# Second stage of a convolution and spectral-mixing kernel: eight single banks, the two array halves a step apart, and the last mixing groups in separate banks

## The chip, the cores and the metric

The kernel runs on one core of one Trainium2 chip. The metric is the device time of one execution in microseconds (us); the median of three runs of the kernel before is 186.36 us (186.29 to 186.38).

## The reference

`x` has 8 batches, 3264 positions and 192 channels; all is float32 at the interface. Each of eight channel groups gets a causal convolution of seven taps (a softmax of `weight`). The result is then mixed in the frequency domain: its lowest 64 frequencies are multiplied by one complex 192 x 192 matrix each, transformed back and added; last comes a channel product with a ReLU.

```python
out = np.einsum('hk,bskhg->bshg', softmax(weight), x_unf)      # causal conv, 7 taps
X = np.fft.rfft(out, axis=1)[:, :64]
Yr = einsum('bmd,mde->bme', Xr, w_r) - einsum('bmd,mde->bme', Xi, w_i)
Yi = einsum('bmd,mde->bme', Xr, w_i) + einsum('bmd,mde->bme', Xi, w_r)
y = np.fft.irfft(Y, n=3264, axis=1)
u = out + y
return u + np.maximum(u @ w_ch, 0.0)
```

## The kernel before

The schedule is written out by hand: each engine executes its instructions in the order of the text, and a library places the semaphores.

The front part loads `x` through GpSimd's queue, convolves it on TensorE with banded matrices (`conv_pass`, line 299), adds and subtracts the two half sequences (`fold`), and transforms them to 64 frequencies (`dft`, `xtrans`). Transposed copies of the convolved rows go to `ct`, cosine and sine tables to `gtab`.

Mixing goes over 16 groups of four frequencies. `mix(g)` (line 472) multiplies by the group's matrices, which stream in through GpSimd's queue into a ring of buffers; twelve small products go to one of two banks `sums`, two groups side by side in a bank. After each second group `mix_copy` (line 479, ScalarE) takes both out to `ymix`, `mix_trans` transposes them (line 485) into a bank of `ye`, and two copies (line 491 on VectorE, 493 on ScalarE) scatter them into `yet`. `keep_busy` (line 570) issues products whose results nobody reads.

The second stage works on 52 items `(q, kk)`: a pair `q` of batches and a block `kk` of 2 x 128 positions. In an item, `a` is 0 or 1 for even and odd positions; each `a` has a PSUM bank of 384 columns (two batches of 192 channels). Into each bank go, for `u @ w_ch`,

- "c": three products of 192 columns, the transposed rows `ct` by the channel matrix (`wa`, `wb`),
- "g": one product of 384 columns, the table `gtab` by `zw[0]`, the mixed spectrum already multiplied by `w_ch`,

then the ReLU in place (`relu`, line 545, ScalarE), then

- "y": one product of 384 columns, `gtab` by `zw[1]`, the mixed spectrum itself, added to the clamped values,

and at last `finish` (line 551, VectorE) adds the convolved rows, writes to one of seven buffers `outs`, and a store goes out on SyncE's queue (line 561).

Every one of these products uses 64 of the array's 128 rows. Half of the terms lie in the lower 64 rows (`row` 0) and half in the upper 64 (`row` 1), so that two products run at once. The two halves must not write to one bank at the same time. `both(n, first, which)` (products on line 538) therefore issues pairs: the lower half adds to bank `first`, the upper half to the other bank of the item; later the halves change banks. Where they change, a wait on TensorE's own semaphore is put ahead (the "turn"). An item holds two banks, so four items are in PSUM at once (`Z[n % 4]`, two tiles named `outleft` and two `outright`). The order per step is

```python
both(n, 0, "c", begin=True); both(n, 0, "g")
both(n - 2, 1, "y", end=True); finish(n - 2)
both(n, 1, "c"); both(n, 1, "g"); relu(n)
both(n - 1, 0, "y")
```

The spectrum times `w_ch` and the spectrum itself, `zw`, are computed by `zw_pair(q, ...)` (lines 498, 499: 384 columns, first 128 rows, then 64) and scaled out by VectorE (line 504) and ScalarE (506). Pairs 0 and 1 come before the first item, pairs 2 and 3 between the first items. The "c" products of items 0 and 1 are issued ahead, while the last two mixing groups wait for weights.

Of the kernel before, what the change touches and what calls it, by code (L numbers as in the profile page):

```python
# [9 lines left out]
ALU = mybir.AluOpType  # L10
# [9 lines left out]
def kernel(  # L20
# [443 lines left out]
    ye = hand_out("right", "mix", (1, 1))  # L464
    trans_banks(2)

    def mix(g):
        yp = sums[(g // 2) % 2][:, D * (g % 2):D * (g % 2) + D]
        for j in range(3):
            for p4 in range(4):  # L470
                m = 8 * (g // 2) + g % 2 + 2 * p4
                nc.tensor.matmul(yp[32 * p4:32 * p4 + 2 * B, :], xt[:, j, :, m],  # L472
                                 wbuf(g)[:, p4, j, :], start=(j == 0), stop=(j == 2),
                                 tile_position=(0, 32 * p4), skip_group_check=True)
        if g >= NWC:
            load_w(g + NWA)

    def mix_copy(d):
        nc.scalar.copy(out=ymix[d % 2][:], in_=sums[d % 2][:, 0:2 * D].rearrange("p (g d) -> p g d", g=2))

    def mix_trans(d):
        et = ye[d % 2][:, :].bitcast(BF16)[:, 0:4 * P].rearrange("p (t g k) -> p t g k", t=2, g=2)
        for t in range(2):
            for g in range(2):
                nc.tensor.transpose(et[:, t, g, :], ymix[d % 2][:, g, 64 * t:64 * t + P], ident[:])
        for t in range(2):
            dst = yet[:, t, :, :].rearrange("p b (r c j) -> p r c b j", r=2, c=2)[:, :, :, :, 4 * d:4 * d + 4]
            srcv = et[:, t, :, :].rearrange("p g (q k) -> p g q k", q=4)[:, :, :, 0:16].rearrange(
                "p g q (c b) -> p g c b q", c=2)
            if t == 0:  # L490
                nc.vector.tensor_copy(out=dst, in_=srcv)
            else:
                nc.scalar.copy(out=dst, in_=srcv)

    def zw_pair(q, zt, engines):
        for i in range(2):
            b = 2 * q + i
            nc.tensor.matmul(zt[:, i, 0:2 * D], yet[:, 0, b, :], wa[:], start=True, stop=False)  # L498
            nc.tensor.matmul(zt[:, i, 0:2 * D], yet[64:P, 1, b, :], wb[64:P, :], start=False, stop=True)  # L499
        for i in range(2):  # L500
            dst = zw[:, :, 2 * q + i, :]
            srcv = zt[:, i, 0:2 * D].rearrange("p (t d) -> p t d", t=2)
            if engines[i] == "v":
                nc.vector.tensor_scalar(out=dst, in0=srcv, scalar1=ascale[:, 0:1], scalar2=None, op0=ALU.mult)  # L504
            else:
                nc.scalar.activation(out=dst, in_=srcv, func=ACT.Copy, scale=ascale[:, 0:1])  # L506

    Z = []
    items = [(q, kk) for q in range(NQ) for kk in list(range(1, NS)) + [0]]
    N = len(items)  # L510

    def pieces(n, a, row, which):
        q, kk = items[n]
        r = slice(64 * row, 64 * row + 64)
# [9 lines left out]
    def both(n, first, which, begin=False, end=False):  # L524
        zt = Z[n % 4]
        lists = (pieces(n, first, 0, which), pieces(n, 1 - first, 1, which))
        old = held.get(n % 4)
        if old is not None and old[0] != first and not begin:
            nop = nc.tensor.nop()
            for name in old[1]:  # L530
                tc.add_manual_dep(nop.ins, name, mybir.DependencyInfo(mybir.DependencyClass.Sync,
                                                                      mybir.DependencyReason.DATA),
                                  reason="row tiles take turns on a bank")
        last = [None, None]
        for k in range(len(lists[0])):
            for row in range(2):
                cols, l, r = lists[row][k]
                m = nc.tensor.matmul(zt[:, first ^ row, cols], l, r, start=(begin and k == 0),  # L538
                                     stop=(end and k == len(lists[row]) - 1), skip_group_check=True)
                last[row] = m.ins.name  # L540
        held[n % 4] = (first, last)

    def relu(n):
        z = Z[n % 4][:, :, 0:2 * D]
        nc.scalar.activation(out=z, in_=z, func=ACT.Relu)  # L545

    def finish(n):
        q, kk = items[n]
        zt = Z[n % 4]
        o = outs[n % NO]  # L550
        nc.vector.tensor_tensor(out=o[:, :, :, :].rearrange("p i a d -> p a i d"),  # L551
                                in0=zt[:, :, 0:2 * D].rearrange("p a (i d) -> p a i d", i=2),
                                in1=c_rows(q, kk), op=ALU.add)
# [9 lines left out]
    def c_ahead(n):  # L563
        for first in range(2):
            both(n, first, "c", begin=(first == 0))

    def keep_busy(n, bank):

# [1 line left out]
            nc.tensor.matmul(sums[bank][:, 0:2 * D], ident[:], xall[:, 0, 0, 0:2, :], start=True, stop=True,  # L570
                             skip_group_check=True)

    AHEAD = 2
    for g, beside in enumerate((0, 1, 1, 2, 2, 2, 1, 2, 2, 2, 2, 2, 2, 2, 0, 0)):
        d = g // 2
        mix(g)
        if g == NG - 2:
            Z += hand_out("left", "out", (2, 2))
            c_ahead(0)
            keep_busy(5, 0)  # L580
        if g == NG - 1:
            mix_copy(d)
            c_ahead(1)
            mix_trans(d)
            keep_busy(4, 0)
        elif g % 2:
            mix_copy(d)
            trans_banks(beside)
            mix_trans(d)
        else:  # L590
            trans_banks(beside)
        if g == NG - 3:
            trans_banks(len(tjobs))
        if NG // 2 <= g < NG - 2:
            keep_busy(3, 1 - d % 2)
    stacks.pop("right").close()
    stacks.pop("sum").close()
    Z += hand_out("right", "out", (2, 2))
    zw_pair(0, Z[2], "va")
    zw_pair(1, Z[3], "va")  # L600
    for n in range(N + 2):
        if n < N:
            if n >= AHEAD:
                both(n, 0, "c", begin=True)
            both(n, 0, "g")
        if 0 <= n - 2 < N:
            both(n - 2, 1, "y", end=True)
            finish(n - 2)
        if n < N:
            if n >= AHEAD:  # L610
                both(n, 1, "c")
            both(n, 1, "g")
            relu(n)
        if n == 1:
            zw_pair(2, Z[2], "va")
        if 0 <= n - 1 < N:
            both(n - 1, 0, "y")
        if n == 1:
            zw_pair(3, Z[3], "va")
    for side in ("right", "left"):  # L620
        stacks[side].close()

# [29 lines left out]
```

## Time and profile before

| | us |
|---|---|
| median of three runs | 186.36 |
| the profiled execution | 186.3 |
| its span, first to last instruction | 184.5 |
| TensorE busy | 157.1 |
| VectorE busy | 119.1 |
| ScalarE busy | 108.7 |

The granted TensorE clock is 0.986 on average over the span. PE is TensorE's products, PEld its weight loads, DVE VectorE, ACT ScalarE, POOL GpSimd, SP SyncE. A timeline row gives start, duration (several instructions that follow each other are merged), engine, line, operation, output and inputs, shapes, count, and in brackets the idle time before it and what ended it. Matrix products are pipelined: a record's duration reaches from its start to the end of the last column's way through the array, and the next product on the same rows starts well before that.

### The profile page before, as it was taken

Reading aid. Unit: us, or ns where it says so; the run is one execution under the profiler, and the core shown is the slowest. Engines: PE = TensorE matmul, PEld = TensorE weight load, DVE = VectorE, ACT = ScalarE, POOL = GpSimd, SP = SyncE. Lnnn points to the kernel's source line nnn. Section 1 sums busy time; section 2 is a strip of 40 time slices with the busy share of each in tenths; the row PEclk is TensorE's granted clock in tenths of the full one; section 3 lists DMA queues with packets and bytes.
Section 4 is the critical chain, followed back from the end, with each engine's and each line's share of the span. In section 5 each row is a group of like instructions: output and inputs, shape, how many; then the busy total and the mean of one; then the engine's idle time right before and its main releaser. Section 6 shows DMA issues by size and latency. Waiting matters only on the chain.

```text
span 184.5 us, 6555 instructions
## 1 busy us (share of the span) xinstructions
PE 157.1 (85%) x2841; PEld 117.1 (63%) x2841; DVE 119.1 (65%) x185; ACT 108.7 (59%) x155; POOL 64.4 (35%) x106
## 2 busy tenths in 40 slices
PE   0064997599999999899998889999999999999970
PEld 0053996499899898678765532566666666666630
DVE  3883865546868866965443303678777877778780
ACT  6367474358686686568645315566666666666640
POOL 7977999576756653332252000000000000000000
PEclk9999999879999999999999999999999999999997
DMA  3999999999999999999999900188879888798884
GB/s 20 176 189 190 190 194 187 191 191 192 191 192 189 202 205 208 204 207 207 209 203 208 171 7 0 66 322 317 326 277 358 319 295 335 290 342 319 319 338 156
DMA packets 50320, 40.14 MB, mean 218 GB/s; under 512 B 29044, under 2 KB 50292, under 8 KB 50292
## 3 DMA queue, kind: packets, MB, share of 16 engines
q0 software_dynamic: 36208, 19.67, 77.5%
q1 hardware_dynamic: 14084, 20.06, 29.6%
q8 instruction: 22, 0.36, 0.8%
q14 instruction: 6, 0.05, 0.1%
HBM read 39.33 MB, written 20.05 MB: 322 GB/s over the span
## 4 chain that ended last, share of the span: by engine, by line
DMA 40%; PE 37%; POOL 14%; issue 4%; DVE 1%; ACT 1%; POOLq 0%; DVEq 0%
DMA xall<-in_x_dram 18%; PE outright L538 17%; PE outleft L538 17%; DMA arena<-in_moe_w_i_dram 12%; DMA ct<-in_moe_w_i_dram 11%; POOL xall L154 10%; POOL ct L280 1%; DVE mixa L504 1%; ACT mixa L506 1%; PE outright L498 1%; PE outright L499 1%; DVE arena L551 1%; PE sumright L472 1%; POOL wa L247 0%; POOL perm L247 0%
## 5 line engine op out<-in xcount | busy, mean ns | idle before, releaser
L299 PEld LDWEIGHTS <-band 128*64 128x64 bf16 x944 | 40.0, 123 | 19.1 <-ACT band L219 11.0
L299 PE MATMUL cvleft<-xall,band 128*64 128x192 bf16 (+4 forms) x640 | 31.9, 254 | 14.7 <-ACT band L219 11.0
L154 POOL DMA_DIRECT2D xall<-in_x_dram x48 | 36.0, 762 | 8.6 <-DMA xall<-in_x_dram 7.3
L538 PEld LDWEIGHTS <-ct 64*128 64x128 bf16 x624 | 24.5, 94 | 21.9 <-PE outleft L538 7.5
L538 PE MATMUL outleft<-mixa,gtab 64*128 64x384 bf16 x208 | 32.0, 323 | 0.5 <-ACT mixa L506 0.3
L538 PE MATMUL outright<-mixa,gtab 64*128 64x384 bf16 x208 | 31.8, 323 | 0.4 <-ACT outright L545 0.3
L323 ACT CAST xall<-cvleft 128x768 bf16<-128x768 f32 (+3 forms) x29 | 21.5, 756 | 10.5 <-PE cvleft L299 10.3
L328 DVE TENSOR_TENSOR arena<-xall 128x1536 bf16<-128x1536 bf16 (+1 forms) x28 | 22.5, 844 | 7.9 <-ACT xall L323 7.5
L545 ACT ACTIVATE outright<-outright 128x768 f32<-128x768 f32 x26 | 20.7, 795 | 10.8 <-PE outright L538 10.8
L545 ACT ACTIVATE outleft<-outleft 128x768 f32<-128x768 f32 x26 | 20.6, 794 | 10.2 <-PE outleft L538 10.2
L551 DVE TENSOR_TENSOR arena<-outright,xall 128x768 f32<-128x768 f32 x23 | 22.0, 958 | 5.7 <-ACT outleft L545 2.9
L551 DVE TENSOR_TENSOR arena<-outleft,xall 128x768 f32<-128x768 f32 x22 | 21.1, 958 | 5.8 <-ACT outright L545 2.6
L375 DVE COPY ct<-trleft 128x1024 bf16<-128x1024 bf16 (+1 forms) x19 | 12.4, 663 | 15.4 <-PE trleft L406 8.7
L538 PEld LDWEIGHTS <-gtab 64*128 64x128 bf16 x416 | 18.9, 94 | 2.6 <-issue 1.1
L538 PE MATMUL outright<-wa,ct 64*128 64x192 bf16 x208 | 17.4, 245 | 0.2 <-ACT mixa L506 0.2
L538 PE MATMUL outleft<-wa,ct 64*128 64x192 bf16 x208 | 17.4, 245 | 0.1
L299 PE MATMUL cvright<-xall,band 128*64 128x192 bf16 (+4 forms) x304 | 15.6, 245 | 1.9 <-DVE xall L321 1.2
L373 ACT COPY ct<-trleft 128x1024 bf16<-128x1024 bf16 x13 | 13.2, 1013 | 5.1 <-PE trleft L403 3.0
L323 ACT CAST xall<-cvright 128x768 bf16<-128x768 f32 (+3 forms) x13 | 9.8, 751 | 8.6 <-PE cvright L299 8.4
L403 PEld LDWEIGHTS <-xall 128*128 128x128 bf16 x208 | 11.7, 98 | 2.6 <-issue 0.3
L538 PE MATMUL outright<-wb,ct 64*128 64x192 bf16 x104 | 12.8, 243 | 0.0
L538 PE MATMUL outleft<-wb,ct 64*128 64x192 bf16 x104 | 12.8, 243 | 0.0
(107 smaller groups left out, 189.5 us busy)
## 6 DMA issues: line engine op xcount, KB each, us to landing
out_dram<-arena SPq DMA_DIRECT2D x41, 384.0 KB, 3.3
xall<-in_x_dram POOLq DMA_DIRECT2D x48, 192.0 KB, 7.8
out_dram<-band SPq DMA_DIRECT2D x7, 384.0 KB, 3.9
ct<-in_moe_w_r_dram POOLq DMA_DIRECT2D x8, 288.0 KB, 9.1
ct<-in_moe_w_i_dram POOLq DMA_DIRECT2D x8, 288.0 KB, 10.0
arena<-in_moe_w_r_dram POOLq DMA_DIRECT2D x8, 288.0 KB, 10.1
arena<-in_moe_w_i_dram POOLq DMA_DIRECT2D x8, 288.0 KB, 11.0
out_dram<-arena SPq DMA_DIRECT2D x8, 144.0 KB, 2.4
```

The costliest lines, as they stand in the source:

```text
L154: nc.gpsimd.dma_start(out=xall[:, q, t % 2, k:k + 4, :], in_=src)
L280: nc.gpsimd.dma_start(out=wbuf(g)[64 * half:64 * half + 64, :, :, :], in_=src[m0:m0 + 7:2, :, :].rearrange("m (p j) e -> p m j e", j=3))
L299: nc.tensor.matmul(o, bd3[:, h, c0:c0 + P - 1:2], xall[:, q, t, ks:ks + n, GRP * h:GRP * h + GRP], start=(main and a == 0), stop=not main, ...
L323: nc.scalar.copy(out=dst, in_=srcv)
L328: nc.vector.tensor_tensor(out=cpm[:, r, :, 0:2 * nb, :], in0=src[:, :, :, 0, :], in1=src[:, :, :, 1, :], op=op)
L373: nc.scalar.copy(out=out, in_=in_)
L375: nc.vector.tensor_copy(out=out, in_=in_)
L403: nc.tensor.transpose(o, cv[:, blk, 0:P], ident[:])
L472: nc.tensor.matmul(yp[32 * p4:32 * p4 + 2 * B, :], xt[:, j, :, m], wbuf(g)[:, p4, j, :], start=(j == 0), stop=(j == 2), tile_position=(0, ...
L538: m = nc.tensor.matmul(zt[:, first ^ row, cols], l, r, start=(begin and k == 0), stop=(end and k == len(lists[row]) - 1), skip_group_check ...
L545: nc.scalar.activation(out=z, in_=z, func=ACT.Relu)
L551: nc.vector.tensor_tensor(out=o[:, :, :, :].rearrange("p i a d -> p a i d"), in0=zt[:, :, 0:2 * D].rearrange("p a (i d) -> p a i d", i=2), ...
```

## The change

- The eight banks of the second stage are single tiles. Its unit is no longer the item with two banks but the slot, an item's `a`, with one bank (`Z[s % 8]`); there are 104 of them.
- Within a slot the lower half puts in c and g first, then the upper half; then the ReLU; then y from the lower half and y from the upper half. The order among slots is worked out at build time by `second_stage`, which keeps times for both halves, VectorE and ScalarE and always issues the product that can start first. In the steady part the lower half is then at slot s with c and g while the upper half is at slot s - 1, the lower y at s - 3 and the upper y at s - 4.
- ReLU, add and eviction are done per slot, on 384 columns instead of 768. A store still takes a whole item, except for the last item: each half goes out alone, the second from ScalarE's queue.
- The weights `zw` of the first pair are computed by `zw_first` in three banks, 192 columns at a time and on all 128 rows (the lower rows of `yet[:, 1]` are set to zero at the start by one memset). Those of the other six batches are six more slots between the items, each with one wide product on the lower half and two on the upper.
- The last two mixing groups go to different banks of `sums`. The first of the two is copied out (ScalarE) and transposed before the other arrives; the other is copied out by VectorE. Their transposes go to both banks of `ye`, so the two copies into `yet` read different banks. Four c slots are issued ahead as before.
- The short item `kk = 0` is no longer the last of a pair but the third from the end.

```diff
+            nc.vector.memset(yet[0:64, 1, :, :], 0.0)
...
+    def mix_bank(g):
+        return sums[(g // 2 + (g == NG - 1)) % 2]
...
-    def zw_pair(q, zt, engines):
+    def zw_first(q, banks):
+        def part(o, i, t):
+            cols = slice(D * t, D * t + D)
+            nc.tensor.matmul(o, yet[:, 0, 2 * q + i, :], wa[:, cols], start=(t == 0 or i == 0), stop=False, ...)
+            nc.tensor.matmul(o, yet[:, 1, 2 * q + i, :], wb[:, cols], start=False, stop=True, ...)
         for i in range(2):
+            part(banks[i][:, 0:D], i, 0)
+        for i in range(2):
+            part(banks[2][:, D * i:D * i + D], i, 1)
+        for i in range(2):
+            scaled(zw[:, 0, 2 * q + i, :], banks[i][:, 0:D], "va"[i])
+        scaled(zw[:, 1, 2 * q:2 * q + 2, :], banks[2][:, 0:2 * D]..., "v")
...
-    items = [(q, kk) for q in range(NQ) for kk in list(range(1, NS)) + [0]]
+    NZ = 8
+    items = [(q, kk) for q in range(NQ) for kk in list(range(1, NS - 2)) + [0, NS - 2, NS - 1]]
+    slots = [(n, a) for n in range(len(items)) for a in range(2)]
+    for k, b in enumerate(range(2, B)):
+        slots.insert(9 + 5 * k, (None, b))
+    NC = 4
...
+    def product(s, row, piece, start, stop):
+        old = held.get(s % NZ)
+        if old is not None and not start and old[0] != row:
+            nop = nc.tensor.nop()
+            tc.add_manual_dep(nop.ins, old[1], ..., reason="row tiles take turns on a bank")
+        cols, l, r = piece
+        m = nc.tensor.matmul(Z[s % NZ][:, cols], l, r, start=start, stop=stop, skip_group_check=True)
+        held[s % NZ] = (row, m.ins.name)
...
+    def relu(s):
+        z = Z[s % NZ][:, 0:2 * D]
         nc.scalar.activation(out=z, in_=z, func=ACT.Relu)
...
+        nc.vector.tensor_tensor(out=o[:, :, a, :], in0=Z[s % NZ][:, 0:2 * D]..., in1=c_rows(q, kk)[:, a, :, :], op=ALU.add)
+        if n == len(items) - 1:
+            (nc.scalar if a else nc.sync).dma_start(out=dst, in_=o[:, :, a, :])
+            return
+        if a == 0:
+            return
...
+    TURN, CLAMP, ADD, COPY, SEEN = 560, 1140, 1340, 1400, 750
+
+    def second_stage():
...
+        while ynext[1] < len(yslots):
+            best = None
+            for row in range(2):
...
+                if t is not None:
+                    best = min(best or (1e9,), (max(t, free[row]), 0, row))
+                s, k = at[row]
+                if s < n_slots:
+                    t = 0 if k else (opened if row == 0 else below)[s]
+                    if t is not None:
+                        best = min(best or (1e9,), (max(t, free[row]), 1, row))
...
         if g == NG - 2:
-            Z += hand_out("left", "out", (2, 2))
+            nc.scalar.copy(out=ymix[d % 2][:, 0, :], in_=mix_bank(g)[:, 0:D])
+            Z += hand_out("left", "out", (1, 1, 1, 1))
             c_ahead(0)
-            keep_busy(5, 0)
-        if g == NG - 1:
-            mix_copy(d)
-            c_ahead(1)
-            mix_trans(d)
+            for t in range(2):
+                mix_trans(LAST, t, (0,), ye[1 - t])
             keep_busy(4, 0)
+        elif g == NG - 1:
+            nc.vector.tensor_copy(out=ymix[d % 2][:, 1, :], in_=mix_bank(g)[:, D:2 * D])
+            c_ahead(2)
+            for t in range(2):
+                mix_trans(LAST, t, (1,), ye[1 - t])
+            keep_busy(4, 1)
...
-    Z += hand_out("right", "out", (2, 2))
-    zw_pair(0, Z[2], "va")
-    zw_pair(1, Z[3], "va")
-    for n in range(N + 2):
...
+    Z += hand_out("right", "out", (1, 1, 1, 1))
+    zw_first(0, Z[4:7])
+    second_stage()
```

More of the change, by code (lines that the diff above doesn't have):

```diff
@@ L495, in zw_pair, with mix_trans @@
-    def zw_pair(q, zt, engines):
+    def mix_trans(d, t, groups=(0, 1), bank=None):
+        et = (bank or ye[d % 2])[:, :].bitcast(BF16)[:, 2 * P * t:2 * P * (t + 1)].rearrange("p (g k) -> p g k", g=2)
+        for g in groups:
+            nc.tensor.transpose(et[:, g, :], ymix[d % 2][:, g, 64 * t:64 * t + P], ident[:])
+        if groups[-1] == 0:
+            return
+        rows = slice(64 * t, P)
+        dst = yet[rows, t, :, :].rearrange("p b (r c j) -> p r c b j", r=2, c=2)[:, :, :, :, 4 * d:4 * d + 4]
+        srcv = et[rows, :, :].rearrange("p g (q k) -> p g q k", q=4)[:, :, :, 0:16].rearrange(
+            "p g q (c b) -> p g c b q", c=2)
+        if t == 0:
+            nc.vector.tensor_copy(out=dst, in_=srcv)
+        else:
+            nc.scalar.copy(out=dst, in_=srcv)
@@ new lines, in scaled @@
+    def scaled(dst, srcv, engine):
+        if engine == "v":
+            nc.vector.tensor_scalar(out=dst, in0=srcv, scalar1=ascale[:, 0:1], scalar2=None, op0=ALU.mult)
+        else:
+            nc.scalar.activation(out=dst, in_=srcv, func=ACT.Copy, scale=ascale[:, 0:1])
+    def zw_first(q, banks):
+        def part(o, i, t):
+            cols = slice(D * t, D * t + D)
+            nc.tensor.matmul(o, yet[:, 0, 2 * q + i, :], wa[:, cols], start=(t == 0 or i == 0), stop=False,
+                             skip_group_check=True)
+            nc.tensor.matmul(o, yet[:, 1, 2 * q + i, :], wb[:, cols], start=False, stop=True,
+                             skip_group_check=True)
@@ L513, in pieces @@
+    slots = [(n, a) for n in range(len(items)) for a in range(2)]
+    for k, b in enumerate(range(2, B)):
+        slots.insert(9 + 5 * k, (None, b))
+    NC = 4
+    def pieces(s, row, which):
+        n, a = slots[s]
+        r = slice(64 * row, 64 * row + 64)
+        if n is None:
+            sides = ((0, wa),) if row == 0 else ((0, wa), (1, wb))
+            return [(slice(0, 2 * D), yet[r, t, a, :], w[r, :]) for t, w in sides]
         q, kk = items[n]
-        r = slice(64 * row, 64 * row + 64)
@@ L522 @@
     held = {}
[L524 to L528, printed above, removed]
-            nop = nc.tensor.nop()
[L530 to L547, printed above, removed]
+    def product(s, row, piece, start, stop):
+        old = held.get(s % NZ)
+        if old is not None and not start and old[0] != row:
+            nop = nc.tensor.nop()
+            tc.add_manual_dep(nop.ins, old[1], mybir.DependencyInfo(mybir.DependencyClass.Sync,
+                                                                    mybir.DependencyReason.DATA),
+                              reason="row tiles take turns on a bank")
+        cols, l, r = piece
+        m = nc.tensor.matmul(Z[s % NZ][:, cols], l, r, start=start, stop=stop, skip_group_check=True)
+        held[s % NZ] = (row, m.ins.name)
@@ new lines, in c_ahead, with second_weights @@
+    def c_ahead(s0):
+        for first in range(2):
+            for k in range(3):
+                for row in range(2):
+                    s = s0 + (first ^ row)
+                    product(s, row, pieces(s, row, "c")[k], first == 0 and k == 0, False)
+    def relu(s):
+        z = Z[s % NZ][:, 0:2 * D]
+        nc.scalar.activation(out=z, in_=z, func=ACT.Relu)
+    def second_weights(s, engine):
+        q, i = divmod(slots[s][1], 2)
+        scaled(zw[:, :, 2 * q + i, :], Z[s % NZ][:, 0:2 * D].rearrange("p (t d) -> p t d", t=2), engine)
@@ L588 @@
             trans_banks(beside)
-            mix_trans(d)
+            for t in range(2):
+                mix_trans(d, t)
         else:
```

113 lines of the change are left out of this document (62 added, 51 removed).

## The prediction

> **What bounds the kernel now.** I read the chain of work that ended last, then the timeline of the table stage by engine, its start and its end.
>
> ```profile
> DMA 40%; PE 37%; POOL 14%; issue 4%; DVE 1%; ACT 1%; POOLq 0%; DVEq 0%
> 107.69 0.46 PE L472 MATMUL sumright<-arena,mixa 128*16 128x192 bf16 x12 [0.63 <-DMA arena<-in_moe_w_i_dram]
> 117.24:177.08 59.84, 59.84 (x986) 39.45 (x982) 46.94 (x49) 39.28 (x50) 0.00 (x0) 1.00 0.84 310
> GB/s 20 176 189 190 190 194 187 191 191 192 191 192 189 202 205 208 204 207 207 209 203 208 171 7 0 66 322 317 326 277 358 319 295 335 290 342 319 319 338 156
> ```
>
> Transfers and their issues (DMA, POOL) bound the front part: PE still waits for weights when the last mixing starts at 107.69. Up to there the change only adds one memset on VectorE, which the chain does not touch. From about 108 us PE carries the chain. In the steady stretch (the third row, a stretch's length and then PE, PEld, DVE, ACT, POOL, clock, DMA share, GB/s) 49 adds take 59.84 us, 1.22 us for an item; DVE is busy 46.94 and ACT 39.28 of it, and the clock is full. One period of PE:
>
> ```profile
> 141.08 0.33 PE L538 MATMUL outright<-mixa,gtab 64*128 64x384 bf16 x2
> 141.24 0.33 PE L538 MATMUL outleft<-mixa,gtab 64*128 64x384 bf16 x2
> 141.47 0.34 PE L538 MATMUL outright<-wa,ct 64*128 64x192 bf16 x4
> 141.65 0.25 PE L538 MATMUL outright<-wb,ct 64*128 64x192 bf16 x2
> 141.73 0.33 PE L538 MATMUL outright<-mixa,gtab 64*128 64x384 bf16 x2
> 141.89 0.33 PE L538 MATMUL outleft<-mixa,gtab 64*128 64x384 bf16 x2
> 142.06 0.33 PE L538 MATMUL outright<-wa,ct 64*128 64x192 bf16 x4
> 142.22 0.25 PE L538 MATMUL outright<-wb,ct 64*128 64x192 bf16 x2
> 142.30 0.33 PE L538 MATMUL outright<-mixa,gtab 64*128 64x384 bf16 x2
> ```
>
> Products come in pairs, lower and upper half of the array at once. A wide pair (384 columns) occupies its halves for 0.163 us (141.08 to 141.24, 141.73 to 141.89), three narrow pairs (192) for 0.245 (142.06 to 142.30). An item is six narrow and four wide pairs: 2 x (0.245 + 2 x 0.1625) = 1.14 us. The other 0.08 us of the 1.22 sit in one place: from 141.24 + 0.16 to 141.47 the array waits for a turn. The wide pair that began at 141.08 must be through before the other half may add to its bank at 141.47, 0.39 us start to start, and only one wide pair lies in between. After that wait three narrow pairs take 0.26 instead of 0.245: about 0.01 to load weights that could not be loaded ahead.
>
> **The change, part by part.** *Steady stage.* A slot is half an item: one bank, three narrow and two wide products on each half of the array, 0.570 us. The built order staggers the halves. The lower half runs c, c, c, table, relu'd table; the upper half enters the bank one slot later and finishes its relu'd product (y) four slots later. Two turns stay in each slot. For the first, a lower wide y (0.163) and one narrow product lie between, so the upper half starts 0.39 - 0.325 = 0.065 us behind the lower and keeps that offset. For the second, three narrow products on the lower half cover 0.16 + 0.245 = 0.41 against 0.39. Both are covered with almost nothing to spare, so the 0.08 us per item goes, and 0.01 us of reloading per turn may remain: between 0 and 2 x 0.01 x 104 = 2.1 us. I take 0.8, because a half that falls behind finds its turn done and its weights loaded.
>
> Behind a waiting weight load, all later products of both halves are queued, so this must fit in both. The rest of the loop has room: from a slot's first product to its free bank it is about 0.41 + 0.23 + 0.41 + 0.21 + 0.48 + 0.05 + 0.16 + 0.23 + 0.16 + 0.27 + 0.56 = 3.2 us of products, turns, relu and add, and eight banks give 8 x 0.57 = 4.6.
>
> ```profile
> 61.09 0.95 DVE L321 CAST xall<-cvright 128x768 bf16<-128x768 f32 x1
> 61.95 0.68 DVE L375 COPY ct<-cvleft 128x1024 bf16<-128x1024 bf16 x1
> L321 DVE CAST xall<-cvright x5: 558/958/1158, 16.9 to 65.7; 128x768 bf16<-128x768 f32 x3, 128x384 bf16<-128x384 f32 x1, 128x960 bf16<-128x960 f32 x1
> 141.67 0.96 DVE L551 TENSOR_TENSOR band<-outleft,xall 128x768 f32<-128x768 f32 x1 [0.26 <-ACT outleft L545]
> ```
>
> *Adds and relus in halves.* No 384-element add is in the trace. The L321 cast out of PSUM takes 0.558 at 384 and 0.958 at 768, and the add takes 0.96 at 768, so I take 0.56 for a half add: 104 x 0.56 = 58.2 us on DVE, up 8 us from 52 x 0.96. A half relu I put at the 0.48 us of ACT's 128x384 copy (below), 50 us in all. Both fit within a slot of 0.57, DVE barely; but a DVE instruction that is ready starts before its predecessor's record ends (61.95 against 61.09 + 0.95), so its own limit is nearer 0.47.
> The Trainium skill (TensorEngine Tiling (Array Packing), PSUM Bottleneck) says the opposite of this edit: after a tiling speedup the PSUM copies may become the bound, and accesses should be vectorised across tiles. The trace agrees that the fixed part is paid twice (2 x 0.558 for 0.958) and does not show the pace; by the rule DVE would set it, which is a rival below.
>
> *Halves out of step.* Row tiles run only in lockstep in this trace. The nearest rows are column tiles: 16 products in step, and 16 whose second half trails (the 4th to 5th ends step by 0.05, not 0.08 or 0):
>
> ```profile
> 63.08 0.83 PE L299 MATMUL cvright<-xall,band 128*64 128x192 bf16 x16
> 64.80 0.36 PE L299 MATMUL cvright<-xall,band 128*64 128x192 bf16 x4
> 64.80 0.41 PE L299 MATMUL cvright<-xall,band 128*64 128x192 bf16 x5
> 64.80 0.85 PE L299 MATMUL cvright<-xall,band 128*64 128x192 bf16 x16
> ```
>
> 0.85 against 0.83: staggering costs the lag once. Bounds for row tiles: nothing, or up to a narrow product's 0.03 us per slot if each entry costs a reload (3 us). I take nothing, since the column rows are the nearest. The Trainium skill (same page, Key Properties) says that tiles work independently and load weights and multiply in parallel, which gives the same zero; no row here shows it for row tiles.
>
> *From the last weights to the first table product.*
>
> ```profile
> 108.74 0.25 PE L538 MATMUL outleft<-wb,ct 64*128 64x192 bf16 x2
> 108.92 0.40 PE L485 MATMUL mixright<-ident,ymix 128*128 128x128 bf16 x4
> 109.15 0.81 PE L570 MATMUL sumright<-xall,ident 128*128 128x384 bf16 x4
> 110.12 0.32 PE L498 MATMUL outright<-wa,yet 128*128 128x384 bf16 x1
> 110.37 0.33 PE L499 MATMUL outright<-wb,yet 64*128 64x384 bf16 x1
> ...
> 112.63 0.34 PE L538 MATMUL outleft<-mixa,gtab 64*128 64x384 bf16 x2 [0.33 <-ACT mixa L506]
> ```
>
> ```profile
> 108.25 0.48 ACT L479 CAST ymix<-sumright 128x384 bf16<-128x384 f32 x1 [3.56 <-PE sumright L472]
> 109.68 0.27 ACT L493 COPY yet<-mixright 128x128 bf16<-128x128 bf16 x1 [0.95 <-DVE yet L491]
> 112.00 0.58 ACT L506 ACTIVATE mixa<-outright,ascale 128x384 bf16<-128x384 f32 x1 [2.06 <-DVE mixa L504]
> ```
>
> ```profile
> 109.36 0.29 DVE L491 COPY yet<-mixright 128x128 bf16<-128x128 bf16 x1 [4.42 <-PE mixright L485]
> 111.35 0.62 DVE L504 TENSOR_SCALAR mixa<-outright,ascale 128x384 bf16<-128x384 f32 x1 [1.70 <-PE outright L499]
> ```
>
> Before, this takes 112.63 - 107.69 = 4.94 us. The copy of the mixed half shortens (0.36 on DVE, estimated from the slope of L321, for 0.48 on ACT), but PE is on its early products until 108.8, so the transposes stay at 108.92. Two of them instead of four: the filler L570 starts 0.11 earlier and ends at 109.69. The two copies into `yet`, which followed each other on one bank (109.36, 109.68), run side by side in two and end by 109.55. So the weights' first product starts at 109.7 instead of 110.12. It was a train of 384-column products at 0.26 apart (110.12, 110.37), alternating between 128 and 64 rows; now it is 192 columns on all 128 rows, some 0.08 apart as in the filler's 0.16 for 384. Two banks are done at 110.2; half-width copies (0.62 - 0.20 and 0.58 - 0.16 = 0.42) run in parallel and end at 110.7; the first table product starts at about 110.8. That is 1.86 us earlier; with the copies still one after the other 1.4.
>
> *Other weights between items.* The two pairs in the middle of the old stage become six slots on row tiles: one wide product below, two above, 12 x 0.1625 = 1.95 us on the upper half, the longer one.
>
> *End.*
>
> ```profile
> 177.14 0.89 PE L538 MATMUL outright<-mixa,gtab 64*128 64x384 bf16 x6
> 177.51 0.80 ACT L545 ACTIVATE outright<-outright 128x768 f32<-128x768 f32 x1 [0.43 <-PE outright L538]
> 178.36 0.73 PE L538 MATMUL outright<-mixa,gtab 64*128 64x384 bf16 x4 [0.32 <-ACT outright L545]
> 178.13 2.02 DVE L551 TENSOR_TENSOR arena<-outright,xall 128x768 f32<-128x768 f32 x2
> 180.15:184.54 4.39, 0.00 (x0) 0.00 (x0) 0.00 (x0) 0.00 (x0) 0.00 (x0) 0.79 0.45 152
> out_dram<-arena SPq DMA_DIRECT2D x41, 384.0 KB, 3.3
> out_dram<-arena SPq DMA_DIRECT2D x8, 144.0 KB, 2.4
> ```
>
> After the last upper table product: 0.17 until it is through, 0.04 to ACT (177.14 + 0.33 against 177.51), relu 0.48, 0.05 back (177.51 + 0.80 against 178.36), a turn 0.39: 1.13 us. After the last y 0.17, 0.10 to DVE (141.24 + 0.33 against 141.67) and an add of 0.56: 0.83. From the last add (178.13 + 2.02 = 180.15) to the end it was 4.39 us with two small stores issued in a row. Now one 192 KB store from ACT's queue comes last, between the two rows of stores (2.4 and 3.3 us), in pieces half as long: +0.1, from -0.3 to +0.5.
>
> *Sum, first table product to last add:* 100 slots x 0.570 + 4 x 0.325 (their early products are done) = 58.3; weights 1.95; the first turn 0.39; stalls while the first slots fill, walked through the order, 0.5 (0.2 to 1.0); reloads 0.8; 1.13; 0.83. Together 63.9, before 180.15 - 112.63 = 67.5: 3.6 less. In all -1.86 - 3.6 + 0.1 = -5.4: span 184.5 to 179.2. The profiled run took 186.3, 1.8 beside its span, which gives 180.9; the median is 0.06 above that run: **181.0 us**.
>
> **Rivals.** *Turns not covered (slower).* The place is the weight load of the upper half, twice in a slot. If a turn takes more than 0.39 when the other half keeps running, everything behind it waits. One gap like the old one (0.08) in every slot costs 104 x 0.077 - 0.8 = 7.2: 188.2. The point is 5.3/104 = 0.05 us per slot. For it: no spare. Against it: the same wait was 0.39 in each period. Chance 0.10.
> *Evictions bind (slower),* the skill's rule as a mechanism: if a half add can neither overlap its predecessor nor have its wait done ahead, its pace is 0.56 + 0.10 = 0.66, 0.08 over my slot: +8.5, 189.5; the point is a pace of 0.63. Against it stands the 61.09/61.95 overlap. Chance 0.05.
> *Part cover.* Reloads or a stagger penalty of 0.03 us per slot: +3, 184.1. Chance 0.11 (182.2 to 185.5).
> *Stores bind.* If 322 GB/s is the most the stores get, an item stays at 1.22 and 52 x 0.065 = 3.4 of the gain goes: 184.3. Slices of 358 speak against it; 0.39 MB in 1.15 us needs 341. Chance 0.04.
> *No change* by several of these together: 0.02.
>
> **Numbers.** The forecast (180.0 to 182.2) has 0.68. The range 180.0 to 184.5 leaves out the slow rivals. Faster by over 0.2%, about what a measurement of this kernel can tell: 0.68 + 0.11 + 0.04 = 0.83; within 0.02; slower 0.15.
>
> **What would show it.** Adds 0.57 to 0.58 us apart, no PE gap over 0.02 in steady state, the first table product at 110.8, the last add at about 174.7. Adds at 0.62 or more with weight loads waiting on PE would prove the turns, with DVE busy throughout the evictions.

## The result: 183.10 us, a gain of 3.2 where 5.4 was forecast

| | before | after |
|---|---|---|
| median of four runs, us | 186.32 (185.72 to 186.38) | 183.10 (182.89 to 183.39) |
| ratio of the times | | 0.9835 (95%: 0.9809 to 0.9861) |
| span of the profiled execution, us | 184.5 | 181.6 |

The time lies in the range (180.0 to 184.5) and the direction was right; the forecast (180.0 to 182.2) was missed. Four stretches add up to the span. B reaches from the first product of the last mixing group to the first table product, C from there to the end of the last add, D from there to the end.

| us, profiled execution | before | after | difference | forecast |
|---|---|---|---|---|
| start to the last group | 107.69 | 109.10 | +1.41 | 0 |
| B | 4.94 | 3.37 | -1.57 | -1.86 |
| C | 67.52 | 64.82 | -2.70 | -3.6 |
| D | 4.39 | 4.31 | -0.08 | +0.1 |

The stretches give 2.94 us where 5.36 were forecast. The missing 2.4 are 1.4 in front of the second stage, 0.3 in B and 0.9 in C, less 0.2 in D.

The windows of the changed kernel: a stretch, its length, the busy time and count of PE, PEld, DVE, ACT and POOL, then clock, DMA share and GB/s. The rows are B, C, D, and 40 us of the steady stage:

```profile
109.10:112.47 3.37, 2.93 (x40) 1.79 (x40) 1.26 (x4) 0.68 (x2) 0.00 (x0) 1.00 0.00 0
112.47:177.29 64.82, 64.10 (x1034) 41.26 (x1033) 57.84 (x108) 49.99 (x107) 0.00 (x0) 1.00 0.82 300
177.29:181.60 4.31, 0.00 (x0) 0.00 (x0) 0.00 (x0) 0.00 (x0) 0.00 (x0) 0.84 0.53 184
134.00:174.00 40.00, 40.00 (x680) 24.23 (x676) 37.70 (x68) 32.15 (x68) 0.00 (x0) 1.00 0.89 326
```

PE still carries the second stage, at full clock. VectorE was busy 46.94 of 59.84 us before (78%); it is now busy 37.70 of 40 (94%). The costliest groups give the unmeasured durations: the half add takes 0.555 us (taken: 0.56), the half relu 0.477 (taken: 0.48).

```profile
L581 DVE TENSOR_TENSOR arena<-outleft,xall 128x384 f32<-128x384 f32 x47 | 25.4, 555 | 4.2 <-PE outleft L558 3.1
L571 ACT ACTIVATE outright<-outright 128x384 f32<-128x384 f32 x52 | 24.5, 477 | 6.9 <-PE outright L558 1.5
```

The pace is that of VectorE's timeline, where equal instructions are merged:

```profile
150.34 2.33 DVE L581 TENSOR_TENSOR arena<-outleft,xall 128x384 f32<-128x384 f32 x4
152.71 2.33 DVE L581 TENSOR_TENSOR arena<-outright,xall 128x384 f32<-128x384 f32 x4
```

Four adds take 152.71 - 150.34 = 2.37 us: 0.592 for a slot, where 0.61 (half of 1.22) was before and 0.570 plus 0.008 of reloading was forecast.

**The front, and an edit that the prediction did not read.** The prediction said that up to the last group "the change only adds one memset". It also changes the order of the transposes and copies for every ordinary pair of mixing groups. Before, all four transposes came first and the two copies behind them; now each half of the transposes is followed by its own copy, and all four still go to one bank of `ye`:

```diff
-    def mix_trans(d):
...
-        for t in range(2):
-            for g in range(2):
-                nc.tensor.transpose(et[:, t, g, :], ymix[d % 2][:, g, 64 * t:64 * t + P], ident[:])
-        for t in range(2):
...
+    def mix_trans(d, t, groups=(0, 1), bank=None):
...
+        for g in groups:
+            nc.tensor.transpose(et[:, g, :], ymix[d % 2][:, g, 64 * t:64 * t + P], ident[:])
...
             if t == 0:
                 nc.vector.tensor_copy(out=dst, in_=srcv)
             else:
                 nc.scalar.copy(out=dst, in_=srcv)
...
-            mix_trans(d)
+            for t in range(2):
+                mix_trans(d, t)
```

Timeline rows of one such pair, before and then after. A bracket is the idle time before a row and what ended it:

```profile
93.22 0.39 PE L485 MATMUL mixright<-ident,ymix 128*128 128x128 bf16 x4
```

```profile
95.14 0.28 PE L489 MATMUL mixright<-ident,ymix 128*128 128x128 bf16 x2
95.46 0.29 DVE L497 COPY yet<-mixright 128x128 bf16<-128x128 bf16 x1
95.80 0.27 PE L489 MATMUL mixright<-ident,ymix 128*128 128x128 bf16 x2 [0.38 <-DVE yet L497]
```

The second two transposes now wait until VectorE has read the first two out of the same bank. VectorE must first get through the copies into `ct` in its queue, and the mixing products behind the transposes on PE wait too. Among the waits from the start of the mixing to the last group, the largest of PE's products is a new one. Before:

```profile
PE sumright L472 <- DMA arena<-in_moe_w_i_dram: 2.3, 4, 0.7
```

After (total, times, longest):

```profile
PE mixright L489 <- DVE yet L497: 4.4, 7, 0.9
```

From there it reaches the transfers. A load into the ring of weight buffers is issued when a mixing product has freed the buffer. GpSimd's issue that waits longest for that, before and then after:

```profile
90.69 0.61 POOL L280 DMA_DIRECT2D arena<-in_moe_w_r_dram  x1 [5.90 <-PE sumright L472]
```

```profile
92.60 0.61 POOL L281 DMA_DIRECT2D arena<-in_moe_w_r_dram  x1 [6.63 <-PE sumright L476]
```

It comes 1.9 us later, although in this execution the mixing began 1.43 us earlier (78.47 for 79.90). From its first product to the last group's, the mixing takes 30.63 us instead of 27.79; how much of that is the order's, the runs below show.

### The profile page after: what moved, and what is told of

Read it like the earlier page. It is cut to its first block, busy times and chain, and to the rows that moved or that the text cites. A ratio compares the mean times of both kernels' runs of the same rounds, so it can differ in the third digit from the quotient of the medians.

```text
span 181.6 us, 6776 instructions
## 1 busy us (share of the span) xinstructions
PE 153.3 (84%) x2850; PEld 115.3 (63%) x2850; DVE 126.3 (70%) x240; ACT 115.6 (64%) x207; POOL 65.0 (36%) x106
## 5 line engine op out<-in xcount | busy, mean ns | idle before, releaser
L558 PE MATMUL outright<-mixa,gtab 64*128 64x384 bf16 x208 | 49.9, 323 | 0.1
L558 PE MATMUL outleft<-mixa,gtab 64*128 64x384 bf16 x208 | 49.5, 323 | 0.2 <-ACT mixa L505 0.2
L558 PEld LDWEIGHTS <-ct 64*128 64x128 bf16 x624 | 33.8, 94 | 14.1 <-PE outleft L558 6.2
L571 ACT ACTIVATE outright<-outright 128x384 f32<-128x384 f32 x52 | 24.5, 477 | 6.9 <-PE outright L558 1.5
L571 ACT ACTIVATE outleft<-outleft 128x384 f32<-128x384 f32 x52 | 24.2, 475 | 6.5 <-PE outleft L558 2.0
L581 DVE TENSOR_TENSOR arena<-outleft,xall 128x384 f32<-128x384 f32 x47 | 25.4, 555 | 4.2 <-PE outleft L558 3.1
L558 PE MATMUL outright<-wa,ct 64*128 64x192 bf16 x208 | 27.3, 246 | 0.0
L558 PE MATMUL outright<-wb,ct 64*128 64x192 bf16 x104 | 24.4, 243 | 0.0
L581 DVE TENSOR_TENSOR arena<-outright,xall 128x384 f32<-128x384 f32 x43 | 23.5, 556 | 1.2 <-PE outright L558 0.2
L558 PE MATMUL outleft<-wb,ct 64*128 64x192 bf16 x104 | 23.9, 243 | 0.0
```

What stands on the lines that cost most here:

```text
L558: m = nc.tensor.matmul(Z[s % NZ][:, cols], l, r, start=start, stop=stop, skip_group_check=True)
L581: nc.vector.tensor_tensor(out=o[:, :, a, :], in0=Z[s % NZ][:, 0:2 * D].rearrange("p (i d) -> p i d", i=2), in1=c_rows(q, kk)[:, a, :, :], ...
```

## The experiments

The theory after this comparison: the alternating order costs the front about 1.4 us, the awaited weight loads 0.021 us per slot, and the filler in front of the weights 0.3. Rivals: the front differs from run to run only; the evictions or the stagger of the halves set the slot. The kernel before was timed beside each run; it took 186.79 beside the first four and 186.50 beside the others, so ratios are compared. A ratio can still shift by 0.004 between sets of runs: "adds split" below has the changed kernel's stretches within 0.13 us and 0.9795 for its 0.9835. The stretches of all runs, from their profiled executions, in us:

| | last group at | B | C | D | slot | ratio (95%) |
|---|---|---|---|---|---|---|
| before | 107.69 | 4.94 | 67.52 | 4.39 | 0.61 | 1 |
| after | 109.10 | 3.37 | 64.82 | 4.31 | 0.592 | 0.9835 (0.9809-0.9861) |
| transposes first | 108.12 | 3.37 | 64.82 | 4.39 | 0.592 | 0.9743 (0.9699-0.9787) |
| before, alternating | 108.96 | 5.49 | 67.50 | 4.96 | 0.61 | 1.0104 (1.0057-1.0150) |
| longer turns | 109.30 | 3.37 | 63.54 | 4.53 | 0.5725 | 0.9766 (0.9726-0.9805) |
| adds split | 108.97 | 3.37 | 64.95 | 4.21 | 0.592 | 0.9795 (0.9763-0.9827) |
| one filler | 109.28 | 2.92 | 64.87 | 4.79 | 0.592 | 0.9824 (0.9784-0.9863) |
| one bank | 107.66 | 3.49 | 64.85 | 4.35 | 0.592 | 0.9777 (0.9742-0.9812) |
| three mends | 107.54 | 2.92 | 63.54 | 4.58 | 0.5725 | 0.9705 (0.9665-0.9745) |
| mends, tuned | 107.50 | 2.92 | 62.78 | 4.59 | 0.5725 | 0.9637 (0.9607-0.9668) |

**Transposes first.** The changed kernel with the old order for the ordinary pairs:

```diff
-            for t in range(2):
-                mix_trans(d, t)
+            for part in "tc":
+                for t in range(2):
+                    mix_trans(d, t, parts=part)
```

Here `"t"` stands for the transposes and `"c"` for the copies.

> The changed kernel, but for each ordinary pair of mixing groups all four transposes are issued first and then the two copies into yet, as in the kernel before. Theory (the alternating order makes TensorE wait in the middle of each of seven pairs for VectorE's copy out of the same bank): from the first mixing product to the last group's first product 27.8 us again instead of 30.6, the last group at 106.3 to 107.7, time 183.1 - 2.6 = 180.5. Rival (the later weights are an accident of that run's transfers): the stretch stays at 30 us or more and the time at 183.1.

It took 182.35 us where 180.5 was expected, ratio 0.9743. Its four times (181.40 to 182.47) all lie below the four of the changed kernel (182.89 to 183.39): 0.75 us of the expected 2.6. The wait for VectorE's copy is gone, and the largest wait of PE's products is again for the transfers, as before:

```profile
PE sumright L476 <- DMA arena<-in_moe_w_i_dram: 3.4, 5, 0.9
```

```profile
108.12 0.47 PE L476 MATMUL sumright<-arena,mixa 128*16 128x192 bf16 x12 [0.71 <-DMA arena<-in_moe_w_i_dram]
```

The mixing takes 28.93 us, not the 27.8 of before: it started earlier, and now the last weights, not PE, are late. The undone order is therefore worth what the transfers leave of it: 1.0 us at the last group.

**The alternating order alone, in the kernel before.** The copies move into the loop of the transposes:

```diff
                 nc.tensor.transpose(et[:, t, g, :], ymix[d % 2][:, g, 64 * t:64 * t + P], ident[:])
-        for t in range(2):
             dst = yet[:, t, :, :]...
```

> The kernel before with one line of the change alone: two transposes, a copy, two transposes, a copy in each of the eight pairs of mixing groups. Theory of the wait in the mixing stage: the stretch from the first to the last group grows from 27.8 to about 30.7, time 186.3 + 2.5 to 3.0 = 189.0. Rival (accident of transfers): 186.3.

188.69 us, ratio 1.0104 (1.0057 to 1.0150): slower by itself. The mixing takes 30.66 us, the 30.63 of the changed kernel, with the same wait:

```profile
PE mixright L485 <- DVE yet L490: 4.8, 8, 0.9
```

The last group comes at 108.96, and B grows by 0.55, because in this kernel the last pair alternates too. Over all ten profiled executions the last group comes at 108.96 to 109.30 with the alternating order (five) and at 107.50 to 108.12 without it (five). The two groups do not overlap, so the front did not differ from run to run only.

The two groups also end differently. With the alternating order the mixing takes 30.61 to 30.66 us in all five (starts from 78.30 to 78.68), and the last group waits for no transfer: the chain through PE and the copies sets its end. Without it the mixing starts between 77.42 and 79.90 and takes 27.79 to 30.24 us, and in all five the last group waits 0.63 to 0.71 us for the weights: the transfers set its end. So the length of the mixing does not measure the order; the order costs as much as its chain ends after the weights have come, 1.0 to 1.4 us here.

**Longer turns.** The list of products is computed with an assumed distance from one half's last column to the other half's first product on a bank. It goes from 560 to 700 columns; a wide product's 384 take 0.163 us, so that is 0.24 to 0.30:

```diff
-    TURN, CLAMP, ADD, COPY, SEEN = 560, 1140, 1340, 1400, 750
+    TURN, CLAMP, ADD, COPY, SEEN = 700, 1140, 1340, 1400, 750
```

> The changed kernel with the order planned for a turn of 700 columns instead of 560, so that the upper half follows the lower one narrow product later. Theory (each turn is still awaited when its weight load is due, and both halves then load their weights with nothing to cover it, 0.010 twice per slot): adds 0.571 apart instead of 0.592, time 183.1 - 1.5 to 2.0 = 181.4. Rival 1 (VectorE's add of 0.56 with its hand-over sets the pace of 0.59): adds stay 0.59 apart, 183.1. Rival 2 (halves that are out of step cost time by themselves): 0.59 or more, 183.1 or slower.

It took 182.30 us where 181.4 was expected, ratio 0.9766. The times (182.02 to 183.21) overlap those of the changed kernel, but C does not: it is 63.54 in both runs with this list (three mends below is the other) and 64.82 to 64.95 in the five with the old one. The slots differ from the 37th add on: up to there it takes 24.89 us from the first table product in the changed kernel and 24.92 here, from there to the last add 39.37 and 38.06. The changed kernel's waits in the steady 40 us hold one awaited weight load for nearly every slot (67 in 67.6 slots):

```profile
PEld L558 <- PE outleft L558: 5.1, 34, 0.2
PEld L558 <- PE outright L558: 5.0, 33, 0.2
```

With the longer turn none of these is left; two others are all:

```profile
DVE arena L581 <- PE outright L558: 1.2, 1, 1.2
ACT outleft L571 <- PE outleft L558: 0.4, 2, 0.3
```

Timeline rows of one slot on PE and PEld show what such a load costs. The changed kernel:

```profile
149.98 0.32 PE L558 MATMUL outright<-mixa,gtab 64*128 64x384 bf16 x1
150.31 0.42 PE L558 MATMUL outright<-wa,ct 64*128 64x192 bf16 x4
150.39 0.12 PEld L558 LDWEIGHTS <-ct 64*128 64x128 bf16 x4 [0.15 <-PE outleft L558]
150.49 0.24 PE L558 MATMUL outright<-wb,ct 64*128 64x192 bf16 x1
150.57 0.32 PE L558 MATMUL outleft<-mixa,gtab 64*128 64x384 bf16 x1
150.57 0.32 PE L558 MATMUL outright<-mixa,gtab 64*128 64x384 bf16 x1
```

With longer turns:

```profile
149.73 0.32 PE L558 MATMUL outright<-mixa,gtab 64*128 64x384 bf16 x1
150.06 0.39 PE L558 MATMUL outright<-wa,ct 64*128 64x192 bf16 x4
150.06 0.18 PEld L558 LDWEIGHTS <-ct 64*128 64x128 bf16 x4
150.22 0.24 PE L558 MATMUL outright<-wb,ct 64*128 64x192 bf16 x1
150.29 0.32 PE L558 MATMUL outleft<-mixa,gtab 64*128 64x384 bf16 x1
150.31 0.32 PE L558 MATMUL outright<-mixa,gtab 64*128 64x384 bf16 x1
```

Which half a row belongs to follows from the list. In the changed kernel the upper half's awaited load starts at 150.39, and the lower half's second load, which stands behind it in the list, starts only with it, 0.08 after the lower half's first product (150.31). With longer turns the lower half's second load starts together with that first product (150.06). From the first narrow product to the third it is 0.18 us in the one and 0.16 in the other; the two intervals carry the 0.02 by which the slots differ. In the changed kernel the table products of both halves start at the same 150.57: the wait has pulled the halves into step. With longer turns they are 0.01 to 0.02 apart and the slot is 0.5725, within 0.003 of the 0.570 of pure products. Halves that run out of step thus cost nothing that shows.

The turn itself did not get longer. From the lower half's table product to the awaited load for the same bank it is 0.41 us in the changed kernel (149.98 to 150.39) and 0.38 with longer turns (149.73 to 150.11). What the constant changed is the list: in its steady part the upper half's first narrow product now stands behind the lower half's second one, where it stood in front of it. The order on each half is the same.

The Trainium skill (TensorEngine Tiling (Array Packing), Key Properties) says that tiles work independently; these rows agree as far as the running goes; that a load which waits in one half holds the other half too, the sentence does not tell.

**Adds split.** Each add of 384 columns becomes two of 192:

```diff
-        nc.vector.tensor_tensor(out=o[:, :, a, :], in0=Z[s % NZ][:, 0:2 * D]..., in1=c_rows(q, kk)[:, a, :, :], op=ALU.add)
+        for i in range(2):
+            nc.vector.tensor_tensor(out=o[:, i, a, :], in0=Z[s % NZ][:, D * i:D * i + D], in1=c_rows(q, kk)[:, a, i, :], op=ALU.add)
```

> The changed kernel with each add of 384 columns made as two adds of 192. Theory (a ready VectorE instruction starts 0.08 before its predecessor's record ends, so its pace is start to start): two adds need 2 x (0.36 - 0.08) = 0.56 per slot, below the 0.592 of TensorE, time 183.1 to 183.6. Rival (evictions pace the stage by their full records and a hand-over): 2 x 0.36 = 0.72 per slot, 0.13 more, 183.1 + 13 = 196.

```profile
134.00:174.00 40.00, 40.00 (x679) 24.19 (x676) 39.97 (x137) 32.17 (x68) 0.00 (x0) 1.00 0.89 326
```

VectorE's busy time rises from 37.70 to 39.97 of 40 us, and still 68 slots fit, in a C of 64.95 for 64.82. The adds do not set the pace, even with twice as many instructions. The Trainium skill (TensorEngine Tiling (Array Packing), PSUM Bottleneck) advises to vectorise PSUM access across tiles in the same bank, since after a 4x speedup the copies may become the bottleneck. Splitting each access to a bank in two costs no pace here. The change itself turned one access to two banks into two, of which that advice does not speak; the prediction left out its condition of the same bank.

**One filler instead of four** before the first pair's weights:

```diff
-            keep_busy(4, 1)
+            keep_busy(1, 1)
```

> The changed kernel with one filler product instead of four after the last transposes. Theory (the weights' first product waits until the fillers are through, 111.26 to 111.39, not for the copies into yet, which end at 110.91): the first table product 0.3 earlier after the last group's mixing, 3.05 instead of 3.37 us, time -0.3 on the changed kernel. Rival (the copies or the change of array mode set it): 3.37 and no change. If the clock falls for want of work in between, later stages are longer and the time rises.

PE's timeline of the changed kernel, transposes of the last group, filler and first product of the weights:

```profile
110.33 0.28 PE L489 MATMUL mixright<-ident,ymix 128*128 128x128 bf16 x2
110.45 0.81 PE L670 MATMUL sumright<-xall,ident 128*128 128x384 bf16 x4
111.42 0.24 PE L511 MATMUL outright<-wa,yet 128*128 128x192 bf16 x1
112.47 0.32 PE L558 MATMUL outleft<-mixa,gtab 64*128 64x384 bf16 x1 [0.23 <-ACT mixa L505]
```

The copies into `yet` were through before the filler was:

```profile
110.60 0.29 DVE L497 COPY yet<-mixright 128x128 bf16<-128x128 bf16 x1 [0.56 <-PE mixright L489]
110.65 0.26 ACT L499 COPY yet<-mixright 64x128 bf16<-64x128 bf16 x1 [2.77 <-PE mixright L489]
```

They end at 110.91, the filler at 111.26, the weights start at 111.42. With one filler the product waits for the copy (110.83 + 0.26 is 1.81 after the last group's start at 109.28; the prediction had 1.86 for the end of the copies):

```profile
111.15 0.24 PE L511 MATMUL outright<-wa,yet 128*128 128x192 bf16 x1 [0.19 <-ACT yet L499]
```

B falls from 3.37 to 2.92. The time (0.9824, interval 0.9784 to 0.9863) cannot resolve 0.45 us, so this stands on the trace alone.

**One bank.** Transposes first, and the last two groups in one bank with serial copies, as in the kernel before:

```diff
-        return sums[(g // 2 + (g == NG - 1)) % 2]
+        return sums[(g // 2) % 2]
...
-            for t in range(2):
-                mix_trans(LAST, t, (0,), ye[1 - t])
-            keep_busy(4, 0)
+            keep_busy(5, 0)
...
-            nc.vector.tensor_copy(out=ymix[d % 2][:, 1, :], in_=mix_bank(g)[:, D:2 * D])
+            mix_copy(d)
             c_ahead(2)
-            for t in range(2):
-                mix_trans(LAST, t, (1,), ye[1 - t])
-            keep_busy(4, 1)
+            for part in "tc":
+                for t in range(2):
+                    mix_trans(d, t, parts=part)
+            keep_busy(4, 0)
```

> The changed kernel with transposes first (as in e1), and the last two mixing groups in one bank as before: one copy on ScalarE, four transposes into one bank, the two copies into yet one after the other. It undoes the part on separate banks alone. Theory (PE's early products and fillers cover most of it): last group's mixing to first table product 3.45 to 3.5 us instead of 3.37, time as e1 or 0.1 more. Rival (the part is worth its 0.4 us, as the prediction had it): 3.8 us.

B is 3.49, only 0.12 above the separate banks of transposes first; the times, 0.9777 for 0.9743, overlap. So of the 1.57 us by which B got shorter, the separate banks brought 0.12 while four fillers stood behind them. The rest, by difference, belongs to the weights on all 128 rows and the evictions of half the width; these two were not taken apart.

**Three mends**: transposes first, longer turns and one filler together.

```diff
-    TURN, CLAMP, ADD, COPY, SEEN = 560, 1140, 1340, 1400, 750
+    TURN, CLAMP, ADD, COPY, SEEN = 700, 1140, 1340, 1400, 750
...
-            keep_busy(4, 1)
+            keep_busy(1, 1)
```

> The changed kernel with all three: transposes first, turn of 700, one filler. If the three causes add up: last group's mixing bounded by the transfers at 107.7 to 108.1, then 3.05, then 63.5, time 183.1 - 0.75 - 1.3 - 0.3 = 180.7; ratio to the kernel before 0.967. If mending one only uncovers another wait (stores at 341 GB/s, or VectorE): less than half of that.

180.61 us, ratio 0.9705. Against the changed kernel the profiled span falls from 181.6 to 178.6: 1.56 in the front, 0.45 in B, 1.28 in C, +0.27 in D. The transfers, in this stretch the stores, run faster than the 322 GB/s at which a rival put their limit:

```profile
134.00:172.00 38.00, 38.00 (x662) 29.59 (x659) 37.01 (x68) 31.62 (x67) 0.00 (x0) 1.00 0.94 343
```

**Mends, tuned**: the same, with the planner's cost of an add and its delay of a semaphore lowered.

```diff
-    TURN, CLAMP, ADD, COPY, SEEN = 700, 1140, 1340, 1400, 750
+    TURN, CLAMP, ADD, COPY, SEEN = 700, 1140, 1150, 1400, 600
```

> As e7, with the plan's constants for the add and the hand-over lowered from 1340 to 1150 and from 750 to 600 columns, since a ready add starts before its predecessor's record ends. Theory: steady pace stays 0.571 to 0.573, but the first slots and the weights between items fill better, 62.8 instead of 63.5 us from the first table product to the last add: 0.6 under e7. Rival (the plan then asks for banks before the add has freed them): 63.5 or more, no gain on e7.

179.54 us, ratio 0.9637 (0.9607 to 0.9668): faster than both kernels. The steady slot stays at 0.5725; C falls by 0.76, all of it before the 37th add: this comes 24.16 us after the first table product where it was 24.92 with three mends, and from there to the last add both take 38.06. In that part the weights' slots stand between the items. Which of the two constants brought it was not taken apart.

## Why the prediction was right or wrong, by its steps

The direction came out by the mechanism that was forecast, at about half its size per slot: an item takes 2 x 0.592 = 1.18 us for 1.22, where 1.14 to 1.16 was forecast, and PE still carries the stage. Of its signs none came as written: the adds are 0.592 apart (0.57 to 0.58), the first table product comes at 112.47 (110.8), the last add ends at 177.29 (174.7). The time fell where the prediction had "part cover" (182.2 to 185.5), though more than half of what is missing came from the front, which stands in no rival. That the range still holds it is in part luck.

*What bounds the kernel.* Right for the second stage: PE carries it. **Wrong for the front, and this is the largest error.** The step that failed is the sentence that up to the last group "the change only adds one memset": the moved copies were not read, and the front was put at zero. It costs 1.41 us at the last group in the profiled execution and 1.0 by undoing it. Done alone in the kernel before it costs 1.27 at the last group and 0.55 in B, and 1.9 us of the time (0.0104 of 186.79).

*Slot of 0.570, halves out of step.* Right once both turns are covered, 0.5725. In the changed kernel one of them is not, and the slot is 0.592. The rival "turns not covered" is refuted in its price (0.077 per slot): what is not covered costs 0.02. The stagger penalty, one form of the rival "part cover", is refuted by the same 0.5725.

*Reloads.* **Mis-sized.** The bounds were 0 to 2.1 us; 0.8 was taken, since a half that falls behind would find its turn done. The runs show 0.0195 per slot from the 37th add on, 1.3 us in the 67 slots behind it; for the slots in front, no run shows the term alone. It comes from one of the two turns, not from both. The upper half was to start 0.39 - 0.325 = 0.065 us behind the lower one, within a narrow product's 0.08; its awaited load alone starts 0.08 behind (150.31 to 150.39). Nor does that half fall behind alone: the awaited load holds the other half as well, both come into step, and the wait returns in the next slot. So of the rival "part cover" its other form, reloads, came true at two thirds of its 0.03. Of the 0.9 by which C missed, this term makes 0.5. The other 0.4 was not taken apart; the last run, which takes 0.76 out of the part before the 37th add by order alone, points at the stalls while the stage fills, put at 0.5.

*Adds and relus in halves.* Right: 0.555 and 0.477. VectorE's own limit was put nearer 0.47. Where the stage starts, it has a backlog and shows it: from the first start to the fifth it is 1.93 us (114.71 to 116.64), 0.48 for one.

```profile
114.71 2.02 DVE L581 TENSOR_TENSOR arena<-outleft,xall 128x384 f32<-128x384 f32 x4 [1.81 <-PE outleft L558]
116.64 1.01 DVE L581 TENSOR_TENSOR arena<-outright,xall 128x384 f32<-128x384 f32 x2
```

The rival "evictions bind" falls with these rows and with the split adds.

*Last weights to first table product.* Right in kind, 0.3 short (1.57 for 1.86). The step that failed ended the filler at 109.69, its start at 109.04 plus four times 0.163, and started the weights there, 2.0 us after the last group. Their first product waits for the end of the filler's record and 0.16 more: 110.45 + 0.81 = 111.26 and 111.42, 2.32 after the last group. The rows before have the same 0.16 (109.15 + 0.81 = 109.96, and 110.12). With one filler the copies release it, and B is 2.92, below the forecast's 3.1.

The separate banks were put at 0.46 of this (1.86 for 1.4); the run with one bank shows 0.12.

*End.* +0.1 forecast, -0.08 measured, within -0.3 to +0.5; over the other runs of the changed stage D lay between 4.21 and 4.79, so the difference is not resolved.

*Stores bind.* Refuted: 343 GB/s with three mends, for a limit of 322.

## What to carry to other kernels

Read a diff for every call whose order it changes, also away from its subject: a helper that was split into parts made each later write to a bank wait for an earlier read of it. When two streams share one queue, an awaited load that is just covered on paper sets both back, and the lag does not heal; the other stream's next load belongs in front of it. That one place in the list gave the pace of pure products. Filler put in while an engine waited has to be counted again when the wait gets shorter.

## What the runs showed of the hardware

- A weight load that waits for the other half's bank costs 0.02 us per slot when the other half's next load stands behind it: two product intervals of both halves get longer (0.18 for 0.16 together) and the halves come into step. With that load in front they run 0.01 to 0.02 apart at the full pace (0.5725 for 0.570).
- A busy share of 39.97 of 40 us on VectorE was not a bound: ready instructions start before the record of their predecessor ends (0.48 apart at 0.555 each), so a full row of busy time can hide slack.
